# A linear-attention and gated feed-forward kernel: gate differences moved into the output product, two weight sums moved into slab 1, and batch 1's steps reordered

## The chip, the cores and the metric

The kernel runs on one core of a Trainium2 chip. The metric is the device time of one execution in microseconds (us). One profiled execution of each kernel gives a trace; the span in a trace is about 1.8 us shorter than the device time of the same run. The granted clock is the TensorE clock as the trace gives it: 1.00 is full speed, 0.50 half of it. The engines are TensorE (PE, with its weight loads PEld), VectorE (DVE), ScalarE (ACT), GpSimd (POOL) and the sync engine's DMA queue (SPq). "The Trainium skill" is the set of reference pages that is cited by page title below.

## The reference, cut to what matters

```python
# q, k, v: 8 batches x 8 heads x 576 x 64
q_s = softmax(q, over the 64 features)      # "norm": exp, sum, reciprocal, multiply
k_s = softmax(k, over the 576 positions)
kv  = einsum('bhsd,bhse->bhde', k_s, v)
x   = einsum('bhsd,bhde->bhse', q_s, kv)    # as 4608 tokens x 512
h   = x @ w_in                              # 512 -> 2048
g   = h / (1 + exp(-beta * h))
out = g @ w_out                             # 2048 -> 512
```

## The kernel before

The 4608 tokens are cut into 9 slabs of 512. In each slab, **pass 1** computes 16 gate tiles GT (TensorE: 4 matmuls each; ACT: the activation; DVE: a scale by 1/beta). The **output product** then multiplies GT with WOUT. From slab 1 on it does so with seven block products in place of eight (a Strassen-like scheme of 256-wide blocks): it needs sums (GS1, GS2) and differences of gate blocks, and sums and differences of weight blocks. Slab 0 uses the plain product, since the weights are only arriving. The attention of a later batch is woven between these matmuls ("ticks" count them). Names that come back in the profiles: EQ is exp(q), normalised in place; QT is EQ transposed; EQR and QTR are the same for the last 64 positions of each batch; KVD is the normalised kv product; XT is x, the operand of pass 1; TS holds the running sum of the first products; "PS" are PSUM banks, of which z5 and z2 are two.

The gate sums, all on DVE; `jobs` are GS1, GS2, and two differences written over GT:

```python
def g_sums(i0, n):                      # n pairs of tiles (i, i + 8)
    ...
    jobs = (
        (GS1[:, i0:i0 + n, :], g(i0, 0), g(i1, 1), ALU.add, ...),
        (GS2[:, i0:i0 + n, :], GT[:, i0:i0 + n, :], GT[:, i1:i1 + n, :], ALU.add, ...),
        (g(i0, 1), g(i0, 1), g(i0, 0), ALU.subtract, ...),
        (g(i1, 0), g(i1, 0), g(i1, 1), ALU.subtract, ...),
    )
    for o, a, b_, op, r, w in jobs:
        add(DVE, lambda e, ...: e.tensor_tensor(o, a, b_, op), r=r, w=w, war=True)
# in pass 1 of slabs 1 to 8, after tile n has been scaled:
if t and n in (8, 14, 16):
    g_sums(*{8: (0, 4), 14: (4, 3), 16: (7, 1)}[n])
```

The output product. `prod` is 16 matmuls of 256 columns, two for each gate pair, and `at(n)` runs hooks: loads, exponentials and norms of later batches. DVE's order is the order of this code.

```python
at(0)
prod(s, GS1, wsum(0)); prod(z5, gs2(0), wo(1, 1))
TS = PS[s]                                   # DVE
at(1)
TS -= PS[z5]                                 # DVE; frees bank z5 for the fourth product
at(2)
prod(z2, gs2(1), wo(0, 0))
TS -= PS[z2]                                 # DVE; frees bank z2 for the fifth
at(3)
prod(z5, gt(0, 0), wo(0, 1)); copy(z5, 0, 1, ACTE)
at(4)
prod(z2, gt(NG, 1), wo(1, 0)); copy(z2, 1, 0, ACTE)
at(5)
prod(z5, gt(0, 1), wsum(1)); last(z5, 1, 1)  # gt(0, 1) holds a difference
at(6)
prod(z2, gt(NG, 0), wsum(2)); last(z2, 0, 0) # gt(NG, 0) holds a difference
at(7)
```

(condensed; the bodies are cut.) `norm_turn` is a reduction and reciprocal on DVE, a multiply on GpSimd, then a DMA transpose QT<-EQ in the sync queue:

```python
if t == 1:
    on(0, w_diff, 0); on(0, exps, 2); on(0, load, 4); on(1, w_diff, 1)
    on(2, norm_main, 2, 0, 2, POOL)
    on(3, norm_main, 2, 2, 2, POOL)
elif t == 2:
    on(0, exps, 3); on(0, exp_qr)
    on(0, norm_turn, 3, 0); on(2, norm_turn, 3, 2)
    on(3, load, 5); on(3, load_rem, "qrf", qt_h, QRF, 4)
    on(4, exp_q, 4); on(4, casts, 4); on(5, exp_k, 4); on(5, exp_kr, 4)
    on(5, load, 6)
    on(6, norm_turn, 4, 0); on(7, norm_turn, 4, 2)
elif t + 2 < B:                              # slabs 3 to 5
    b = t + 2
    on(0, exps, b); on(0, casts, b)
    if b + 2 < B: on(0, load, b + 2)
    on(3, norm_turn, b, 0); on(4, norm_turn, b, 2)
```

The softmax here doesn't subtract the row's maximum and nothing guards it: scores larger than these inputs give would overflow.

## Time and profile before

| | before |
|---|---|
| device time, median of 3 runs (a fourth came with the result) | 298.32 us (297.19 to 298.73) |
| span of the trace | 296.9 us |
| TensorE busy | 271.1 us, 91% |
| DVE busy | 195.6 us, 66% |

TensorE is the engine that is nearly always busy, so what matters is what it waits for. The view of waits, engine PE, kernel before: who waited, on whose result, the total, how often, and the longest, in us.

```profile
PE PS L695 <- DVE GS L666: 12.4, 9, 2.0
PE PS L373 <- DVE EQ L333: 2.3, 2, 2.1
...
PE PS L695 <- DVE TS L749: 0.4, 1, 0.4
PE PS L373 <- POOL EQ L333: 0.4, 1, 0.4
PE PS L375 <- DMA QT<-EQ: 0.4, 1, 0.4
```

Most of what it waits is one thing: DVE's gate sums, 12.4 us in 9 waits, one in each slab from 1 to 8 (two in slab 3). The timeline of slab 5 shows how. Columns: start, busy time, engine, line, operation, output<-input, number of instructions; in brackets the idle time before and what ended it. TensorE, then DVE:

```profile
192.22 1.69 PE L695 MATMUL PS<-WSUM,GS 128*128 128x256 bf16 x14
195.81 0.39 PE L695 MATMUL PS<-WSUM,GS 128*128 128x256 bf16 x2 [1.90 <-DVE GS L666]
```

```profile
187.04 1.83 DVE L666 TENSOR_TENSOR GS<-GT 128x1024 bf16<-128x1024 bf16 x2
188.90 1.29 DVE L666 TENSOR_TENSOR GT<-GT 128x1024 bf16<-128x1024 bf16 x2
...
192.41 1.43 DVE L666 TENSOR_TENSOR GS<-GT 128x768 bf16<-128x768 bf16 x2
193.87 1.03 DVE L666 TENSOR_TENSOR GT<-GT 128x768 bf16<-128x768 bf16 x2
194.81 0.61 DVE L628 TENSOR_SCALAR GT<-GT,RB 128x512 bf16<-128x512 bf16 x2
195.46 0.63 DVE L666 TENSOR_TENSOR GS<-GT 128x256 bf16<-128x256 bf16 x2
```

The first product needs the GS1 of all eight pairs. TensorE does 14 of its 16 matmuls and stands still for 1.90 us before the last pair. The last activation of the slab ends at 193.11 us, but DVE is then in the burst for pairs 4 to 6. The differences of that burst (193.87, 1.03 us) stand in front of the last two scales and the last GS1, though nothing wants a difference before the sixth product.

The second loss is at the end of slab 0. The same views, kernel before, TensorE and DVE:

```profile
41.03 0.40 PE L373 MATMUL PS<-IDB,EQ 128*128 128x128 bf16 x4 [2.10 <-DVE EQ L333]
```

```profile
37.05 2.36 DVE L677 TENSOR_TENSOR WSUM<-WOUT 128x2048 bf16<-128x2048 bf16 x2 [4.93 <-DMA WOUT<-in_moe_w_out_dram]
39.33 0.68 DVE L331 TENSOR_REDUCE QS<-EQ 128x8 f32<-128x512 bf16 x1
```

Two w sums (2.36 us) wait for the last weights and stand ahead of batch 1's first reduction, and TensorE waits 2.10 us for the normalised EQ. The table by stretches gives the granted clock after that wait. Columns: stretch, its length, PE busy and its matmuls, granted clock (PEclk), DMA share, GB/s:

```profile
41.00:42.00 1.00, 0.96 (x8) 0.96 1.10 346
42.00:43.00 1.00, 0.96 (x3) 0.50 1.10 349
...
44.00:45.00 1.00, 1.00 (x4) 0.50 1.11 351
```

The clock is at 0.50 for about 3 us after TensorE has started again. This trace has a second such stretch, in slab 3, where TensorE had waited 1.96 us for gate sums until 133.14 us; it matters below, when slab 3 is compared:

```profile
134.00:135.00 1.00, 1.00 (x7) 0.54 0.61 141
135.00:136.00 1.00, 1.00 (x7) 0.50 1.09 151
```

### The profile page before, as it was taken

To read this page: it belongs to the slowest core of one execution; us is meant where nothing else is said; L and a number is where in the kernel's file an instruction comes from. 1 tells how busy PE (TensorE), PEld (TensorE's weight loads), DVE (VectorE), ACT (ScalarE), POOL (GpSimd) and SP (SyncE) were. 2 spreads that over 40 slices of the span, in tenths; PEclk is the share of its full clock that TensorE was granted. 3 is DMA by queue.
4 is the path that set the end of the run, shared out by engine and by line. 5 is a ranking of instruction groups with operands and counts; after the bars stand their busy time and mean duration, and the time that the engine had idled before them with its cause. 6 is when DMAs were issued, how large, how long until landed. Compare 5 with 4: busy or idle time off the path is not lost.

```text
span 296.9 us, 4679 instructions
## 1 busy us (share of the span) xinstructions
PE 271.1 (91%) x1820; PEld 169.4 (57%) x1845; DVE 195.6 (66%) x426; ACT 183.8 (62%) x282; POOL 62.9 (21%) x84
## 2 busy tenths in 40 slices
PE   8899979997999899979999799979998999899894
PEld 2444424446854685536755685568546845774483
DVE  5944295399757959795659774977488349625931
ACT  5787356998177978793467847784673477037510
POOL 2870013310800086300830072006000100000000
PEclk9999989999999999997999999999999999999999
DMA  7999999995970059999991044003500030002005
GB/s 227 302 206 194 258 354 348 239 369 189 338 204 0 0 94 334 296 281 228 337 269 61 2 98 171 0 1 81 186 2 0 20 141 0 2 35 106 2 2 140
DMA packets 57174, 45.40 MB, mean 153 GB/s; under 512 B 26416, under 2 KB 56128, under 8 KB 56128
## 3 DMA queue, kind: packets, MB, share of 16 engines
q1 hardware_dynamic: 52320, 40.38, 47.3%
q0 software_dynamic: 4224, 4.19, 8.5%
q10 hardware_dynamic: 608, 0.53, 0.5%
q8 instruction: 14, 0.23, 0.3%
q14 instruction: 8, 0.07, 0.1%
HBM read 36.71 MB, written 9.44 MB: 155 GB/s over the span
## 4 chain that ended last, share of the span: by engine, by line
PE 59%; DVE 23%; DMA 8%; POOL 3%; ACT 2%; SPq 2%; issue 2%; POOLq 0%; DVEq 0%
PE PS L375 32%; PE PS L695 27%; DMA WOUT<-in_moe_w_out_dram 7%; DVE GS L666 7%; DVE GT L628 4%; DVE GT L666 4%; DVE QS L331 2%; SPq L275 2%; ACT GT L622 2%; POOL EQ L333 1%; DMA QT<-EQ 1%; POOL WIN L543 1%; DVE WSUM L677 1%; DVE EQ L333 1%; DVE KVD L417 1%
## 5 line engine op out<-in xcount | busy, mean ns | idle before, releaser
L375 PE MATMUL PS<-XT,WIN 128*128 128x512 bf16 x560 | 129.5, 379 | 2.1 <-DVE XT L455 1.2
L622 ACT ACTIVATE GT<-PS,BETA 128x512 bf16<-128x512 f32 x144 | 98.7, 687 | 41.1 <-PE PS L375 40.9
L375 PEld LDWEIGHTS PS<-XT,WIN 128*128 128x128 bf16 x576 | 52.9, 98 | 60.9 <-DVE XT L455 2.6
L628 DVE TENSOR_SCALAR GT<-GT,RB 128x512 bf16<-128x512 bf16 x144 | 50.1, 374 | 38.1 <-ACT GT L622 37.9
L333 POOL TENSOR_TENSOR EQ<-EQ,QI 128x1024 bf16<-128x1024 bf16 (+1 forms) x16 | 27.0, 1690 | 127.3 <-DVE QI L332 126.9
L695 PE MATMUL PS<-WOUT,GT 128*128 128x256 bf16 x256 | 32.6, 273 | 0.4 <-DVE TS L749 0.4
L666 DVE TENSOR_TENSOR GS<-GT 128x1024 bf16<-128x1024 bf16 (+5 forms) x48 | 31.8, 704 | 0.8
L695 PE MATMUL PS<-WOUT,GS 128*128 128x256 bf16 x256 | 32.0, 280 | 0.2
L695 PE MATMUL PS<-WSUM,GT 128*128 128x256 bf16 x256 | 31.6, 273 | 0.1
L725 ACT COPY O2S<-PS 128x512 f32<-128x512 f32 x16 | 9.4, 584 | 35.2 <-PE PS L695 33.0
L695 PE MATMUL PS<-WSUM,GS 128*128 128x256 bf16 x128 | 17.0, 273 | 12.4 <-DVE GS L666 12.4
L695 PEld LDWEIGHTS PS<-WOUT,GS 128*128 128x128 bf16 x256 | 25.6, 100 | 4.3
L695 PEld LDWEIGHTS PS<-WOUT,GT 128*128 128x128 bf16 x256 | 24.9, 98 | 4.3 <-DVE TS L749 0.7
L695 PEld LDWEIGHTS PS<-WSUM,GT 128*128 128x128 bf16 x256 | 24.9, 98 | 3.7
L733 DVE TENSOR_TENSOR O2S<-TS,PS 128x512 f32<-128x512 f32 x16 | 11.0, 685 | 21.3 <-PE PS L695 21.3
L666 DVE TENSOR_TENSOR GT<-GT 128x1024 bf16<-128x1024 bf16 (+2 forms) x48 | 22.5, 510 | 0.8
L300 ACT ACTIVATE EQ<-QF 128x512 bf16<-128x512 f32 x32 | 17.7, 619 | 8.1 <-DMA QF<-in_q_dram 8.1
L375 PE MATMUL PS<-VB,EK 128*128 128x129 bf16 x128 | 22.1, 220 | 0.5 <-DVE VB L348 0.5
L695 PEld LDWEIGHTS PS<-WSUM,GS 128*128 128x128 bf16 x128 | 11.6, 98 | 17.8 <-DVE GS L666 14.9
L331 DVE TENSOR_REDUCE QS<-EQ 128x16 f32<-128x1024 bf16 (+1 forms) x20 | 19.8, 989 | 0.0
L455 ACT CAST XT<-PS 128x512 bf16<-128x512 f32 x18 | 10.3, 584 | 14.9 <-PE PS L375 11.1
L300 ACT ACTIVATE EK<-KF 128x512 bf16<-128x512 f32 x32 | 18.0, 620 | 0.0
(77 smaller groups left out, 227.8 us busy)
## 6 DMA issues: line engine op xcount, KB each, us to landing
out_dram<-O2S SPq DMA_DIRECT2D x8, 1024.0 KB, 4.3
QF<-in_q_dram SPq DMA_DIRECT2D x6, 1024.0 KB, 7.3
KF<-in_k_dram SPq DMA_DIRECT2D x6, 1024.0 KB, 10.2
VF<-in_v_dram SPq DMA_DIRECT2D x6, 1024.0 KB, 12.2
QF<-in_q_dram SPq DMA_DIRECT2D x4, 512.0 KB, 6.2
KF<-in_k_dram SPq DMA_DIRECT2D x8, 256.0 KB, 6.4
VF<-in_v_dram SPq DMA_DIRECT2D x8, 256.0 KB, 6.5
WIN<-in_moe_w_in_dram POOLq DMA_DIRECT2D x4, 512.0 KB, 7.2
```

Of the source, the lines that this page charges most:

```text
L275: add(SP, lambda e, h=h, a=a: e.dma_start(buf[64 * h:64 * h + 64, :, :], a), w=[(name, h)], slot=f"{name}{h}")
L300: add(ACTE, lambda e, o=o, a=a: e.activation(o, a, ACT.Exp), r=[(name + "f", i, hp)], w=[("e" + name, i, hp)])
L331: add(DVE, lambda e: e.tensor_reduce(s_, a, AX.X, ALU.add), r=ks, w=[("qs", i, hp0)])
L333: add(eng, lambda e: e.tensor_tensor(a, a, vb, ALU.mult), r=ks + [("qi", i, hp0)], w=ks)
L375: add(PE, lambda e: e.matmul(o, l, r_, start=start, stop=stop), r=r, w=w, bank=[bk])
L455: add(eng, lambda e: (e.copy if eng == ACTE else e.tensor_copy)(XT[i][:, hp, :], PS[bk][:, :]), r=[("ps", bk)], w=[("xt", i, hp)], bank=[bk])
L622: add(ACTE, lambda e: e.activation(GT[:, f, :], PS[bk][:, :], ACT.Silu, scale=BETA[:, f:f + 1]), r=[("ps", bk), "beta"], w=[("gt", f, 0), ...
L628: add(DVE, lambda e: e.tensor_scalar(GT[:, f, :], GT[:, f, :], RB[:, f:f + 1], None, ALU.mult), r=k + ["rb"], w=k)
L666: add(DVE, lambda e, o=o, a=a, b_=b_, op=op: e.tensor_tensor(o, a, b_, op), r=r, w=w, war=True)
L695: add(PE, lambda e, l=l, r_=r_, st=st, u=u, i=i: e.matmul(PS[bk][:, 256 * u:256 * u + 256], l, r_, start=st, stop=end and i == NG - 1, ski ...
L725: add(eng, lambda e: (e.copy if eng == ACTE else e.tensor_copy)(o, bank3(bk)), r=[("ps", bk)], w=w, bank=[bk])
L733: add(DVE, lambda e: e.tensor_tensor(o, ts, bank3(bk), ALU.add), r=["ts", ("ps", bk)], w=w, bank=[bk])
```

## The change

The intent: sums only in pass 1, in smaller bursts that end earlier (4, 2, 1 and 1 pairs); the differences as two operations of 128x2048 inside the output product, where DVE has gaps; the two w sums out of the way of batch 1's norms and into slab 1's pass 1; three of batch 1's four normalising multiplies on GpSimd; batch 1's steps at the ticks where their operands arrive; and batch 1's QF in quarters, started after the third WOUT chunk. The diff, cut to its core:

```diff
-        def g_sums(i0, n):          # GS1, GS2 and both differences, n pairs
+        def g_sum1(i, n): ...       # GS1 of n pairs
+        def g_sum2(i, n): ...       # GS2 of n pairs
+        def g_diff(fh):             # one difference, all 8 pairs: 128x2048
+            f, th = NG * fh, 1 - fh
+            add(DVE, lambda e: e.tensor_tensor(gv(f, th, NG), gv(f, th, NG), gv(f, 1 - th, NG),
+                                               ALU.subtract), ...)
@@ pass2_fast
             TS -= PS[z5]
+            g_diff(0)
             at(2)
             prod(z2, *gs2(1), *wo(0, 0), True)
             TS -= PS[z2]
+            g_diff(1)
             at(3)
@@ pass 1
-                    if t and n in (8, 14, 16):
-                        g_sums(*{8: (0, 4), 14: (4, 3), 16: (7, 1)}[n])
+                    for i_, w_ in {8: ((0, 4),), 12: ((4, 2),), 14: ((6, 1),), 16: ((7, 1),)}.get(
+                            n if t else 0, ()):
+                        g_sum1(i_, w_)
+                        g_sum2(i_, w_)
+                    if t == 1 and n in (4, 9):
+                        w_sum(2 * (n == 4))
@@ slab 0
-                todo = [(104 + 5 * hp, steps(t_steps, 1, (hp,), NOW, ACTE)) for hp in range(NHP)]
+                todo = [(x, steps(t_steps, 1, (hp,), NOW, ACTE))
+                        for hp, x in enumerate((98, 104, 109, 114))]
   ... (the ticks of exp_k, cast_v and kv_steps likewise; one kv step from the tail into the product)
-                load_main("qf", qt_h, QF, 1, split=2, after=P.writer[("wout", 7, 0)])
+                load_main("qf", qt_h, QF, 1, split=4, after=P.writer[("wout", 11, 0)])
-                w_sum(0)
-                w_sum(2)
-                    norm_main(1, hp, 1, POOL if hp % 2 else DVE)
+                    norm_main(1, hp, 1, POOL if hp else DVE)
```

More of the change, by code (lines that the diff above doesn't have):

```diff
@@ L647, in store8, with gv, gk, g_sum1 @@
                     r=[("o2", 0, 2 * th + u, dh) for u in range(2)], slot=f"outr{th}{dh}{h}")
-        def g_sums(i0, n):
-            def g(f, th):
-                return GT[:, f:f + n, 256 * th:256 * th + 256]
-            def gk(f, th):
-                return [("gt", f + x, th) for x in range(n)]
-            i1 = i0 + NG
-            jobs = (
-                (GS1[:, i0:i0 + n, :], g(i0, 0), g(i1, 1), ALU.add, gk(i0, 0) + gk(i1, 1),
-                 [("gs1", i0 + x) for x in range(n)]),
-                (GS2[:, i0:i0 + n, :], GT[:, i0:i0 + n, :], GT[:, i1:i1 + n, :], ALU.add,
-                 gk(i0, 0) + gk(i0, 1) + gk(i1, 0) + gk(i1, 1),
-                 [("gs2", i0 + x) for x in range(n)]),
-                (g(i0, 1), g(i0, 1), g(i0, 0), ALU.subtract, gk(i0, 0) + gk(i0, 1), gk(i0, 1)),
-                (g(i1, 0), g(i1, 0), g(i1, 1), ALU.subtract, gk(i1, 0) + gk(i1, 1), gk(i1, 0)),
-            )
-            for o, a, b_, op, r, w in jobs:
-                add(DVE, lambda e, o=o, a=a, b_=b_, op=op: e.tensor_tensor(o, a, b_, op),
-                    r=r, w=w, war=True)
+        def gv(f, th, n):
+            return GT[:, f:f + n, 256 * th:256 * th + 256]
+        def gk(f, th, n):
+            return [("gt", f + x, th) for x in range(n)]
+        def g_sum1(i, n):
+            add(DVE, lambda e: e.tensor_tensor(GS1[:, i:i + n, :], gv(i, 0, n), gv(i + NG, 1, n),
+                                               ALU.add),
+                r=gk(i, 0, n) + gk(i + NG, 1, n), w=[("gs1", i + x) for x in range(n)], war=True)
+        def g_sum2(i, n):
+            add(DVE, lambda e: e.tensor_tensor(GS2[:, i:i + n, :], GT[:, i:i + n, :],
+                                               GT[:, i + NG:i + NG + n, :], ALU.add),
+                r=[k_ for f in (i, i + NG) for th in range(2) for k_ in gk(f, th, n)],
+                w=[("gs2", i + x) for x in range(n)], war=True)
+        def g_diff(fh):
+            f, th = NG * fh, 1 - fh
+            add(DVE, lambda e: e.tensor_tensor(gv(f, th, NG), gv(f, th, NG), gv(f, 1 - th, NG),
+                                               ALU.subtract),
+                r=gk(f, 0, NG) + gk(f, 1, NG), w=gk(f, th, NG), war=True)
         def quarter(fh, dh):
@@ L784, in steps @@
                     return lambda: go(fn(*a))
-                todo = [(104 + 5 * hp, steps(t_steps, 1, (hp,), NOW, ACTE)) for hp in range(NHP)]
-                todo += [(106, one(exp_kr_s, 1))]
-                todo += [(110 + 5 * hp, one(exp_k, 1, hp, 1)) for hp in range(3)]
-                todo += [(122, steps(kv_steps, 1, (0,), NOW)), (126, steps(kv_steps, 1, (1,), NOW))]
-                todo += [(114, one(cast_v, 1, 0, DVE)), (115, one(cast_v, 1, 1, DVE)),
-                         (123, one(cast_v, 1, 2, DVE))]
+                todo = [(x, steps(t_steps, 1, (hp,), NOW, ACTE))
+                        for hp, x in enumerate((98, 104, 109, 114))]
+                todo += [(105, one(exp_kr_s, 1))]
+                todo += [(x, one(exp_k, 1, hp, 1)) for hp, x in enumerate((106, 110, 115))]
+                todo += [(x, one(cast_v, 1, hp, DVE)) for hp, x in enumerate((110, 114, 122))]
+                todo += [(x, steps(kv_steps, 1, (hp,), NOW))
+                         for hp, x in enumerate((116, 121, 126))]
             elif t < 3:
@@ L845, in bass_efficient_attn_shen__then__act_swish_beta_kernel @@
                 go(out_step(1, 0, NOW, ACTE))
-                go(kv_steps(1, (2,), NOW))
                 go(out_step(1, 1, NOW, ACTE))
```

## The prediction

> **What bounds it now.** TensorE is busy 91% of the 296.9 us span (page, busy shares), at a granted clock of 0.99. In every slab from 1 to 8 it stalls once before the last GS1 pair: the group "WSUM,GS" shows 12.4 us idle, all released by the DVE `GS` sums. By slab (TensorE waits per stretch): 1.3, 1.3, 2.1, 1.9, 1.9, 1.4, 1.3, 1.3. The timeline shows why: DVE does four-operation bursts (3.1 us for four pairs, 2.5 us for three), is behind when the last activation lands, and the last GS1 queues behind the 1.03 us of differences. The second loss is slab 0's output product: TensorE waits 2.1 us for batch 1's first normalised EQ, because two w sums (2.36 us) sit before its reduction, then runs at half clock for about 3.4 us (windows: 0.5 from 42 to 45 us).
>
> **Steady slabs (4 to 8).** Two 128x2048 differences should cost 1.22 us each, as the w sums do in the trace (the Trainium skill, "VectorE: DVE Perf Modes", side-by-side section, gives 1224 ns for this size at two elements a cycle; the trace agrees). That is 2.44 instead of 2.8 us, and it leaves the path: in the output product DVE has idle pieces of about 0.8, 0.8, 0.8 and 1.1 us, and the differences are first needed four products later. Replaying DVE's queue with trace durations, it has caught up at the last activation, and GS1 of the last pair comes about when TensorE arrives. Gain 1.75+1.75+1.3+1.25+1.25 = 7.3 us.
>
> **Slab 0.** No w sums before the norms; but batch 1's QF now waits for a later WOUT chunk (lands near 33.4 instead of 30.3 us). DMA is saturated either way, so the last QF lands near 39 us as before, its first quarter near 37. First transpose near 39.1 instead of 41.0, shorter stall, less half clock. Gain 2.3 us.
>
> **Slabs 1 to 3 give back.** Here DVE is full in the product: w differences (slab 1), norm reductions early (1.21 us each). Adding 2.44 us delays both TS subtractions, which release the banks of the 4th and 5th products, and the norms. Also the Trainium skill, "SBUF — State Buffer", section "SBUF: two separate sides", says a GpSimd operation and a two-input DVE operation exclude each other; the trace agrees (a 0.69 us multiply took 0.91 beside GpSimd's), so g_diff waits behind the 1.9 us GpSimd norm. Slab 1: about +2.5 against -0.8 gained. Slab 2: +2.3 against -1.3. Slab 3's first output matmul waits for QT<-EQ by DMA, queued behind about 24 us of saturated loads that start only after slab 2's second norm; that norm comes about 1.4 us later, so TensorE idles several us there, whatever slab 3's sums gain, and restarts at half clock, +1.5. Slabs 1 to 3 together: about +4.5.
>
> **Sum.** -7.3 -2.3 +4.5 = -5: 293.0 us, range 289.5 to 296.0. Chances: faster 0.38, same 0.60, slower 0.02.
>
> **What would show it.** Right: "WSUM,GS" idle falls from 12.4 to below 2.5 us; L666-type differences gone, two 1.2 us ones in each product; slabs 4 to 8 each 1.2 to 1.8 us shorter; slab 0 ends 2 to 3 us earlier. Wrong or right for the give-back: TensorE waits on DVE TS and on POOL EQ in slabs 1 and 2 of 2 us or more each, and a DMA QT<-EQ wait of 3 us or more in slab 3 with clock 0.5 after it.
>
> **What would make it wrong.** If the slab 1 to 3 waits overlap with slack that I count twice, the time goes to 289. If slab 0's later QF misses its transposes, or POOL's three serial multiplies (1.04 us each) pace TensorE, slab 0 gains nothing: 295.

## The result, and the profile after

| | before | changed |
|---|---|---|
| device time, median of 4 runs | 297.97 us (297.19 to 298.73) | 294.40 us (293.82 to 294.99) |
| ratio | | 0.9881, 95% interval 0.9845 to 0.9916 |
| span of the trace | 296.9 us | 292.3 us |
| TensorE busy | 91% | 93% |

A ratio is the mean time of one kernel's fast runs over that of the other's of the same rounds, so it is not quite the ratio of the two medians. The time fell by 3.6 us, 1.2%: inside the predicted range, and within 2%. The two traces differ by 4.6 us, 1 us more than the medians, since the traced run of the kernel before was a slow one of its kind (298.70 us); all differences by slab below are those of the two traces.

The view of waits, engine PE, changed kernel, against the same one of before:

```profile
PE PS L375 <- DMA QT<-EQ: 3.4, 1, 3.4
PE PS L373 <- POOL EQ L333: 2.6, 3, 1.5
PE PS L698 <- DVE TS L757: 2.0, 2, 1.3
PE PS L698 <- DVE GS L656: 1.9, 3, 0.8
PE PS L373 <- DVE EQ L333: 1.4, 1, 1.4
...
PE PS L698 <- DVE TS L752: 0.7, 1, 0.7
```

The wait for gate sums fell from 12.4 to 1.9 us, and 1.6 of these are in slab 1. In their place stand three that were 0.4 us each: the DMA transpose of QT (3.4), the GpSimd norm (2.6) and DVE's TS subtractions (2.7 in both lines).

The same slab 5, changed kernel, TensorE and DVE:

```profile
193.83 2.05 PE L698 MATMUL PS<-WSUM,GS 128*128 128x256 bf16 x16
```

```profile
195.14 0.29 DVE L656 TENSOR_TENSOR GS<-GT 128x256 bf16<-128x256 bf16 x1
...
198.26 1.22 DVE L668 TENSOR_TENSOR GT<-GT 128x2048 bf16<-128x2048 bf16 x1
...
200.59 1.22 DVE L668 TENSOR_TENSOR GT<-GT 128x2048 bf16<-128x2048 bf16 x1
```

All 16 matmuls of the first product run through. The last GS1 (195.14) comes 1.3 us after the product has begun and just before its last pair needs it. The two wide differences take 1.22 us each and lie behind the first and the second TS subtraction, where they hold up nothing. The length of each slab, from the first matmul of its pass 1 to that of the next (start of the first "XT,WIN" group in each timeline):

| slab | before us | changed us | difference |
|---|---|---|---|
| 0 (from 16.01 / 16.21) | 36.48 | 34.69 | -1.8 |
| 1 | 31.62 | 34.41 | +2.8 |
| 2 | 29.50 | 30.58 | +1.1 |
| 3 | 33.31 | 34.56 | +1.3 |
| 4 | 30.34 | 28.41 | -1.9 |
| 5 | 30.34 | 28.41 | -1.9 |
| 6 | 29.79 | 28.29 | -1.5 |
| 7 | 27.74 | 26.42 | -1.3 |
| 8 to the end of the span | 31.77 | 30.32 | -1.5 |

Slabs 4 to 8 gained 8.1 us, slab 0 gained 1.6 (its end moved from 52.49 to 50.90 us), and slabs 1 to 3 gave back 5.1. Slab 2 shows how. DVE, TensorE and GpSimd in its output product, changed kernel:

```profile
104.66 0.69 DVE L752 TENSOR_TENSOR TS<-TS,PS 128x512 f32<-128x512 f32 x1
105.26 1.88 DVE L668 TENSOR_TENSOR GT<-GT 128x2048 bf16<-128x2048 bf16 x1
107.06 1.21 DVE L331 TENSOR_REDUCE QS<-EQ 128x16 f32<-128x1024 bf16 x1
...
108.47 0.63 DVE L757 TENSOR_TENSOR TS<-TS,PS 128x512 f32<-128x512 f32 x1
109.02 2.67 DVE L668 TENSOR_TENSOR GT<-GT 128x2048 bf16<-128x2048 bf16 x1
```

```profile
105.41 1.26 PE L698 MATMUL PS<-WOUT,GT 128*128 128x256 bf16 x10 [0.74 <-DVE TS L752]
...
109.16 0.28 PE L698 MATMUL PS<-WOUT,GT 128*128 128x256 bf16 x1 [1.32 <-DVE TS L757]
```

```profile
104.16 1.90 POOL L333 TENSOR_TENSOR EQ<-EQ,QI 128x1024 bf16<-128x1024 bf16 x1 [20.28 <-DVE QI L332]
108.70 1.90 POOL L333 TENSOR_TENSOR EQ<-EQ,QI 128x1024 bf16<-128x1024 bf16 x1 [2.64 <-DVE QI L332]
```

The second TS subtraction (108.47) stands behind a wide difference of 1.88 us and a reduction of 1.21 us, and TensorE waits 1.32 us for its bank. The wait of 0.74 us before it is not the work of the differences: the first TS subtraction (104.66) stands in front of both. DVE had begun this product with a reduction that waited 1.45 us for ACT's exponential (until 102.50 us), and the 0.74 us are the same in a2, b4 and c2, where the differences come later. Both differences take longer than 1.22 us while a GpSimd multiply runs: the first one starts at 105.26, the multiply ends at 106.06, and the difference ends 1.08 us after that. The second norm's multiply starts at 108.70 us; before the change it started at 106.03.

In slab 3, the first output matmul waits for the DMA transpose, and the granted clock then drops. The half clock is no difference between the two traces, since slab 3 of the kernel before had one too (0.54 and 0.50, shown above); what differs is the wait for QT, 0.39 us before and 3.43 now, and the wait for gate sums, 2.13 us before and 0.28 now:

```profile
139.40 0.39 PE L375 MATMUL PS<-QT,KVD 128*128 128x512 bf16 x1 [3.43 <-DMA QT<-EQ]
```

```profile
139.00:140.00 1.00, 0.60 (x5) 0.95 1.26 306
140.00:141.00 1.00, 1.00 (x7) 0.50 1.04 385
...
142.00:143.00 1.00, 1.00 (x6) 0.50 0.94 197
```

### The profile page after: what moved, and what is told of

The parts are those of the page before. It is cut to its first block, busy times and chain, and to the rows that moved or that the text cites. A ratio compares the mean times of both kernels' runs of the same rounds, so it can differ in the third digit from the quotient of the medians.

```text
span 292.3 us, 4671 instructions
## 1 busy us (share of the span) xinstructions
PE 270.7 (93%) x1820; PEld 169.0 (58%) x1845; DVE 197.8 (68%) x409; ACT 183.8 (63%) x282; POOL 67.2 (23%) x85
## 4 chain that ended last, share of the span: by engine, by line
PE 69%; DVE 12%; DMA 9%; POOL 3%; ACT 3%; SPq 2%; issue 2%; POOLq 0%; DVEq 0%
PE PS L375 41%; PE PS L698 28%; DMA WOUT<-in_moe_w_out_dram 6%; DVE QS L331 3%; DVE GT L668 2%; POOL EQ L333 2%; DMA QT<-EQ 2%; SPq L275 2%; DVE GT L628 1%; ACT GT L622 1%; DMA QF<-in_q_dram 1%; DVE GS L661 1%; POOL WIN L543 1%; DVE QI L332 1%; DVE GS L656 1%
## 5 line engine op out<-in xcount | busy, mean ns | idle before, releaser
L628 DVE TENSOR_SCALAR GT<-GT,RB 128x512 bf16<-128x512 bf16 x144 | 52.5, 382 | 39.6 <-ACT GT L622 39.0
L333 POOL TENSOR_TENSOR EQ<-EQ,QI 128x1024 bf16<-128x1024 bf16 (+1 forms) x17 | 28.2, 1656 | 120.2 <-DVE QI L332 117.0
L698 PE MATMUL PS<-WOUT,GT 128*128 128x256 bf16 x256 | 33.3, 275 | 2.7 <-DVE TS L757 2.0
L668 DVE TENSOR_TENSOR GT<-GT 128x2048 bf16<-128x2048 bf16 x16 | 23.1, 1441 | 0.0
L661 DVE TENSOR_TENSOR GS<-GT 128x512 bf16<-128x512 bf16 (+2 forms) x32 | 22.7, 710 | 0.0
L348 POOL CAST VB<-VF 128x512 bf16<-128x512 f32 x25 | 18.0, 719 | 7.9 <-DMA VF<-in_v_dram 6.1
```

The source lines that it names most:

```text
L333: add(eng, lambda e: e.tensor_tensor(a, a, vb, ALU.mult), r=ks + [("qi", i, hp0)], w=ks)
L348: add(eng, lambda e: (e.copy if eng == ACTE else e.tensor_copy)(o, a), r=[("vf", i, hp), ("vone", i)], w=[("vb", i, hp)])
L628: add(DVE, lambda e: e.tensor_scalar(GT[:, f, :], GT[:, f, :], RB[:, f:f + 1], None, ALU.mult), r=k + ["rb"], w=k)
L661: add(DVE, lambda e: e.tensor_tensor(GS2[:, i:i + n, :], GT[:, i:i + n, :], GT[:, i + NG:i + NG + n, :], ALU.add), r=[k_ for f in (i, i + ...
L668: add(DVE, lambda e: e.tensor_tensor(gv(f, th, NG), gv(f, th, NG), gv(f, 1 - th, NG), ALU.subtract), r=gk(f, 0, NG) + gk(f, 1, NG), w=gk(f ...
L698: add(PE, lambda e, l=l, r_=r_, st=st, u=u, i=i: e.matmul(PS[bk][:, 256 * u:256 * u + 256], l, r_, start=st, stop=end and i == NG - 1, ski ...
```

## The experiments

Twelve runs follow, of ten new kernels and of two once more, in three calls; each call is one chip, on which the kernel before ran too. Theory Q, mine: what slabs 1 to 3 lose is the place of the wide differences in DVE's queue in slabs 1 and 2; they hold up the bank releases and the norms, and slab 2's second norm holds up the loads that stand ahead of slab 3's transposes in the sync queue. Its rivals: the two w sums in slab 1 (W), or a DMA queue that is full whatever slab 2 does (D).

### a1_early2: slab 2's differences back in pass 1

```diff
+                        if t == 2:
+                            g_diff(0, i_, w_); g_diff(1, i_, w_)   # after g_sum2, of the burst's pairs
@@ pass2_fast
-            g_diff(0)   and   g_diff(1)
+            if not (t == 2): g_diff(0)   and likewise g_diff(1)
```

> The changed kernel, with slab 2's gate differences put back into pass 1 beside its sums (all other slabs as changed). Theory Q (DVE's queue in slab 2's product delays the bank releases and the second norm, and through the norm the loads and slab 3's transposes): slab 2's two TS waits (2.0 us) go, a GS wait of about 1.3 us comes back, the second GpSimd norm of slab 2 ends about 2 us earlier against the start of the slab, the QT landing in slab 3 comes as much earlier, its wait falls from 3.4 to about 2 us; time about 2.3 us less than the changed kernel's 294.4, so 292. Rival D (the DMA queue's loads end when they end, whatever slab 2 does): the QT landing does not move, what slab 2 gains is waited again in slab 3, time 294.

Measured: 291.54 us, ratio 0.9792 (0.9754 to 0.9830). Slab 2 is 29.61 us (changed: 30.58), slab 3 is 32.41 (34.56). Both of slab 2's TS waits are gone and a GS wait of 1.3 us is back. The wait for QT hardly fell, to 3.1 us, because TensorE also came earlier; I had expected about 2. But the landing moved, and that is the point on which Q and D differ (it is put side by side with a2 below). The time itself proves less than it seems: this trace has no half clock in slab 3, and the changed kernel without it takes 32.16 us there (e1, below), so slab 3's 2.15 us are not the edit's. Against e1's trace the span is 0.8 us shorter, about what slab 2 gained; that 292 us came out as forecast is in part luck.

### a2_late12: the differences of slabs 1 and 2 behind the norms

```diff
             TS -= PS[z5]
-            g_diff(0)
+            if not (t < 3): g_diff(0)
             ...
             copy(z5, 0, 1, ACTE)
+            if t < 3: g_diff(0)
             ...
             copy(z2, 1, 0, ACTE)
+            if t < 3: g_diff(1)
```

> The changed kernel, with the two wide differences of slabs 1 and 2 moved behind the fourth and fifth product, so behind the TS subtractions and the norm reductions. Theory Q: the TS and POOL EQ waits in slabs 1 and 2 fall from 4.9 us to under 2; slab 2's second norm ends 2 us earlier; the QT wait in slab 3 does not grow; time 291 (3 to 4 us less than 294.4). Rival W (the loss in slab 1 is the two w sums now in its pass 1, not the differences): slab 1 keeps its length of 34.4 us, the time stays within 1 us of 294.4.

Measured: 288.17 us, ratio 0.9668 (0.9632 to 0.9704). Nothing is removed here, four operations stand later in one queue, and the time falls by about 6 us against the 294.4 of the first measurement, or 4 against the 292.0 of the last one (e1). Slab 1 takes 31.33 us instead of 34.41, slab 2 takes 29.40 instead of 30.58, slab 3 takes 33.52 instead of 34.56, with a half clock (0.50 from 135 to 138 us) as in the changed kernel's first trace. The waits for TS and POOL EQ, 5.3 us in the changed kernel's trace, are 1.5 us (this one's trace, view of waits: 0.7 and 0.8; the 0.7 is slab 2's first TS wait, which stays). Rival W alone would have left slab 1 as it was; it does not hold as the main cause.

The norm and the landing, from the timelines of four traces (start of the second GpSimd multiply of slab 2 plus its 1.90 us; start of the first output matmul of slab 3, which in all four waits for QT):

| kernel | second norm ends | first QT matmul | between |
|---|---|---|---|
| before | 107.93 | 137.54 | 29.6 |
| changed | 110.60 | 139.40 | 28.8 |
| a1_early2 | 109.21 | 137.92 | 28.7 |
| a2_late12 | 105.82 | 134.18 | 28.4 |

The landing follows the norm over 4.8 us of shifts, to within 1.3 us. That is what theory Q says, and rival D (a landing that does not move with slab 2) falls.

### a3_turn_first: batch 6's loads behind batch 4's transposes

```diff
-                on(5, load, 6)
                 on(6, norm_turn, 4, 0)
                 on(7, norm_turn, 4, 2)
+                on(7, load, 6)
```

> The changed kernel, with batch 6's loads queued behind batch 4's transposes in slab 2 instead of in front of them. If slab 3's wait for QT is the place of the transposes in the queue: that wait (3.4 us) is gone, TensorE does not fall to half clock there, slab 3 takes about 5 us less, time 289.5; slab 4 keeps its 28.4 us, since batch 6 is needed only at its end. If instead the transposes wait for the norm itself or for the engine, the wait stays above 2 us and the time above 293.

Measured: 291.15 us, ratio 0.9769 (0.9723 to 0.9816), so less than expected. The wait for QT is gone and slab 3 takes 28.97 us, 5.6 less than in the first trace of the changed kernel and 3.2 less than in e1's, which had no half clock. But slab 4, which I had said would keep its 28.41, takes 32.97. The sync queue and TensorE, this kernel:

```profile
118.97 5.94 SPq L482 DMA_TRANSPOSE QT<-EQ  x2
...
154.04 1.27 SPq L489 DMA_TRANSPOSE QTR<-EQR  x1
```

```profile
156.96 0.20 PE L375 MATMUL PS<-QTR,KVD 128*128 128x64 bf16 x1 [2.71 <-DMA QTR<-EQR]
```

Batch 4's transposes are now issued at 118.97 us (134.55 in the changed kernel), but the loads they overtook push batch 7's loads and with them slab 3's own transposes, so that QTR is late in slab 4. The same kind of wait moved one slab on, here with a half clock behind it (0.50 from 158 to 160 us). The trace is of the slowest of the four runs (292.72 us, the others 289.77 to 291.28). The place in the queue was the cause in slab 3; cured in one place only, most of it is lost again in another.

### a4_wsum_home: the two w sums back in slab 0

```diff
-                    if t == 1 and n in (4, 9):
-                        w_sum(2 * (n == 4))
@@ slab 0
                 exp_q(1)
+                w_sum(0)
+                w_sum(2)
```

> The changed kernel, with the two w sums back in slab 0, before batch 1's norms. Theory Q: WOUT's last chunk landed at 36.1 us, so the sums end near 38.6, slab 0's first norm comes about 1 us later and slab 0 is 0.5 to 1.5 us longer; slab 1's GS waits fall from 1.6 to about 0.3 us; the two cancel, time 294 to 295. Rival W (w sums in slab 1 are what it lost): slab 1 falls by 2 us or more, time 293 or less.

Measured: 293.41 us, ratio 0.9843 (0.9806 to 0.9880). Slab 0 takes 35.59 us (+0.9), slab 1 takes 32.58 (-1.8): slab 1's wait for gate sums (1.6 us) is gone, its waits for the norm (2.2) and TS (0.7) are unchanged. So W holds for 1.8 us of slab 1, which slab 0 gives back by half; the time is not clear of the changed kernel's.

### b1_only_gates and b2_only_slab0: the two halves of the change

b1 is the kernel before with the new sums and the wide differences; b2 is the kernel before with everything else.

```diff
# b1, against the changed kernel: slab 0 as before
+ w_sum(0), w_sum(2) after exp_q(1);  - the w_sum calls in slab 1's pass 1
+ split=2, after wout 7;  POOL if hp % 2 else DVE;  the old ticks
# b2, against the changed kernel: gates as before
+ g_sums(...) at n in (8, 14, 16), with both differences;  - g_diff(0), g_diff(1)
```

> The kernel before, with the gate part of the change alone (new sums and the two wide differences; slab 0, its loads and its w sums as before). Theory Q: slab 0 keeps 36.5 us, slab 1 takes about 32.6 (GS wait near 0.2, but TS and POOL waits of 2.5 to 3 us), slabs 2 and 3 about 30.6 and 34.3, slabs 4 to 8 together about 8 us less; time 293 to 294, ratio 0.985: so the whole gain of the change is the gate part and the slab 0 part nets about nothing. Rival: the slab 0 part carries its own 1.6 us, then this run is at 296.

> The kernel before, with everything but the gate part of the change (w sums in slab 1's pass 1, batch 1's norms on GpSimd, its steps by arrival, QF after the third WOUT chunk; sums and differences in pass 1 as before). Theory Q: slab 0 about 1.7 us less, slab 1 longer, because its pass 1 now holds 2.4 us of w sums on top of the differences (GS wait 3 us or more instead of 1.3), the rest as before: time 297.5 to 300, within 2% of before. Rival: the slab 0 part is worth 1.6 us by itself: 296.5.

Measured: b1 291.74 us, ratio 0.9777 (0.9736 to 0.9817), better than I had expected (slab 1, 32.59 us, is as forecast; slab 0 took 35.29 us instead of 36.5, since no half clock followed its wait of 2.01 us); b2 299.23 us, ratio 1.0040 (1.0020 to 1.0061). In b2 slab 0 falls by 1.9 us against before (36.48 to 34.61), and slab 1 grows by 2.7 (31.62 to 34.35), with waits of 2.7 us for gate sums and 0.6 for a w sum, and a half clock (0.50 from 70 to 73 us) that slab 1 of the kernel before did not have. So the rival for b2, 1.6 us won by slab 0's part alone, falls: the w sums cost in slab 1 what their absence saves in slab 0. That b1 seems 2.7 us faster than the whole change, more than b2's 1.2 us can explain, called for a repeat beside it.

### e1_change_again and e2_only_gates_again: the whole change and the gate part in the same rounds

No edit: the changed kernel, and b1's.

> The changed kernel once more, on the same chip and in the same rounds as the gate part alone: 294 us, ratio 0.988 (with the half clock in slab 3 in most runs), or down to 292.7 in runs that escape it.

> The gate part alone again, beside the whole change. If the slab 0 part costs about 1.2 us, as its own run against the kernel before says (1.0040), this is 1 to 2 us faster than the whole change on this chip: ratio near 0.980. If the 2.7 us between the two in the earlier calls was chance of clock and chip, the two agree within 0.5 us.

Measured: 291.96 us, ratio 0.9817 (0.9791 to 0.9843), and 292.37 us, ratio 0.9818 (0.9797 to 0.9839). They agree. The 2.7 us was not the slab 0 part: all four runs of the first measurement had a granted clock of 0.986 or 0.994, and three of the five in this one had 1.000 (291.50 to 291.96 us; the two at 0.994 took 292.85 and 292.93). This trace of the changed kernel has the same wait for QT, 3.22 us, and no half clock after it. Kernel e1_change_again, table by stretches:

```profile
139.00:140.00 1.00, 1.00 (x12) 1.00 1.17 414
140.00:141.00 1.00, 1.00 (x11) 1.00 1.34 393
```

Slab 3 then takes 32.16 us instead of 34.56, with the QT wait 0.2 us shorter. So the ratio of the change was 0.988 and 0.982; whether slab 3's wait is followed by the half clock is a part of that difference, and chip may be another. At equal clock the gain is clearest: in runs at 1.000 the kernel before took 297.18 and 297.32 us and the changed one 291.50 to 291.96. Its slab 0 part adds nothing that these runs can tell.

### d1_no_pool_norm: no GpSimd multiply in slabs 1 and 2 (wrong result)

```diff
+            if b in (2, 3):
+                return
             add(eng, lambda e: e.tensor_tensor(a, a, vb, ALU.mult), ...)
```

> Wrong result on purpose: the changed kernel without GpSimd's normalising multiply for batches 2 and 3 (the reductions and reciprocals stay). If the GpSimd multiply is what stretches the wide differences, all four in slabs 1 and 2 take 1.22 us as in slabs 4 to 8, instead of 1.22, 2.67, 1.88 and 2.67, and TensorE's TS waits in slabs 1 and 2 fall from 2.7 us to about 2 (the wait for the queue itself stays: reduction and difference before the second subtraction). If the stretch has another source (the operands, the DMA), the durations stay above 1.8 us.

One run, for its trace; the result is wrong, as said, and its 285.18 us are no claim. The four wide differences of slabs 1 and 2 in the changed kernel and in this one, DVE timeline:

```profile
71.86 1.22 DVE L668 TENSOR_TENSOR GT<-GT 128x2048 bf16<-128x2048 bf16 x1
...
74.96 2.67 DVE L668 TENSOR_TENSOR GT<-GT 128x2048 bf16<-128x2048 bf16 x1
...
105.26 1.88 DVE L668 TENSOR_TENSOR GT<-GT 128x2048 bf16<-128x2048 bf16 x1
...
109.02 2.67 DVE L668 TENSOR_TENSOR GT<-GT 128x2048 bf16<-128x2048 bf16 x1
```

```profile
71.79 1.22 DVE L670 TENSOR_TENSOR GT<-GT 128x2048 bf16<-128x2048 bf16 x1
...
74.89 1.21 DVE L670 TENSOR_TENSOR GT<-GT 128x2048 bf16<-128x2048 bf16 x1
...
102.61 1.22 DVE L670 TENSOR_TENSOR GT<-GT 128x2048 bf16<-128x2048 bf16 x1
...
105.71 1.21 DVE L670 TENSOR_TENSOR GT<-GT 128x2048 bf16<-128x2048 bf16 x1
```

The stretch is the GpSimd multiply's doing. TensorE's TS waits fall only from 2.7 to 2.0 us, as expected: the blocking accounts for 0.7 us of them, the order in the queue for the rest (0.74 us of which is slab 2's first TS wait, behind the reduction).

This trace also extends the table of shifts. Without the multiply, batch 3's transposes have no norm to wait for: the loads behind them start at 102.60 us instead of 111.91, batch 4's transposes are issued at 126.11 instead of 134.55, no wait for QT is left, and slab 3 takes 28.76 us.

### b3_qf7: QF released by the second WOUT chunk again

```diff
-split=4, after=P.writer[("wout", 11, 0)]
+split=4, after=P.writer[("wout", 7, 0)]
```

> The changed kernel, with batch 1's QF quarters released by WOUT's second chunk, as the halves were before, instead of its third. In the changed kernel TensorE waits 1.4 us for the first normalised EQ and ACT waited until 36.9 us for the first QF quarter. If the later release is what holds the first norm: the quarter lands near 35 us, the wait goes, slab 0 is 1.0 to 1.5 us shorter, time 293. If the copies only share one saturated DMA, the first quarter gains under 1 us and WOUT's last chunk lands later, with no wait for it: time within 0.7 us of 294.4.

Measured: 293.31 us, ratio 0.9838 (0.9794 to 0.9881), not clear of the changed kernel's 0.9817 to 0.9881. The issue of QF moved from 33.59 to 30.20 us (chain of waits), and the first quarter's exponential only from 36.87 to 36.50. Sharing with WOUT ate the head start; slab 0 took 34.55 us against 34.69.

### b4_all and c2_arrival: what the experiments point to

```diff
# b4: a2's late differences, and
-                on(5, load, 6)
+                on(7, load, 6)                       # behind norm_turn(4, 2)
-                    on(0, load, b + 2)
+                    on(7 if t == 3 else 0, load, b + 2)
-                    if t == 1 and n in (4, 9): w_sum(2 * (n == 4))
+                todo += [(115.5, one(w_sum, 2))]     # slab 0
                 go(out_step(1, 3, NOW, DVE))
+                w_sum(0)                             # end of slab 0
# c2: b4, and
-                        for hp, x in enumerate((98, 104, 109, 114))]      # transposes
+                        for hp, x in enumerate((104, 113, 117, 121))]
-                         for hp, x in enumerate((116, 121, 126))]         # kv products
+                         for hp, x in enumerate((123, 125, 127))]
```

> The changed kernel with the differences of slabs 1 and 2 late (as a2), batch 6's loads behind batch 4's transposes and batch 7's loads behind slab 3's transposes (so that the wait which a3 moved to slab 4's QTR does not come back), and the two w sums in slab 0's tail, one after the second cast and one after the last XT cast, where DVE stood idle for 1.2 and 1.9 us. Expected against a2's 288.2: slab 3 33.5 to about 29 us, slab 4 stays at 28.4, slab 1's GS wait of 1.3 goes: time 282 to 283.5, ratio about 0.948. If the DMA is simply too full in slabs 2 to 4 whatever the order, a wait of 2 us or more stays in slab 3 or 4 and the time is above 285.

> b4_all with batch 1's steps in slab 0's output product moved to where their operands arrive in the traces: transposes at ticks 104, 113, 117, 121 instead of 98, 104, 109, 114, the kv products at 123, 125, 127 instead of 116, 121, 126. In b4_all TensorE waited 1.8 us for the first normalised EQ at tick 98. If the stall is only a matter of order, it falls below 0.5 us and the time by about 1.2 us, from 283.7 to 282.5. If the chain behind it (the kv reciprocals, KVD and the XT casts at the end of slab 0) is what ends the slab, slab 0 keeps its 35 us and the time stays within 0.5 us of 283.7.

Measured: b4 283.73 us, ratio 0.9519 (0.9499 to 0.9540); c2 282.49 us, ratio 0.9487 (0.9467 to 0.9507). Both beat both kernels; b4 is just above the 282 to 283.5 us expected. In b4 slab 3 takes 29.15 us and slab 4 stays at 28.41, so the queue was not too full, it was in the wrong order; no DMA wait is among TensorE's. In c2 slab 0 takes 33.34 us (b4: 35.14) and the 1.8 us wait for the first EQ is gone. TensorE's longest waits that are left in c2 are 1.6 us for DVE's XT casts (in two), 1.2 for the very first operand of the kernel and 1.2 for KVD (in three).

## Why the prediction was right, and where its terms were off

- **Slabs 4 to 8: predicted -7.3, measured -8.1 us.** Right in mechanism and nearly in size: the GS wait did not merely shrink, it is zero in these slabs, where I had left up to 0.15 us.
- **The cost of a wide difference: predicted 1.22, measured 1.22 us** in slabs 3 to 8, where no GpSimd multiply stands beside it. The Trainium skill's "VectorE: DVE Perf Modes" gives 1224 ns for this size in its side-by-side section; the trace agrees.
- **Slab 0: predicted -2.3, measured -1.6 us by its end, -1.8 by its length.** This term was mis-sized, and most of what it did measure is the clock. The times that the prediction gave came out: the first quarter of QF at 36.84 us ("near 37"), the first transpose at 39.23 ("near 39.1"), and the wait for the first EQ fell from 2.10 to 1.40 us. But two waits appeared that were not there before, 0.33 us for a norm on GpSimd and 0.52 for ACT's XT cast, so that slab 0's waits inside the product fell only from 2.34 to 2.25 us. The rest is the half clock that did not come: in b1 the old slab 0 without it takes 35.29 us (before 36.48, changed 34.69), so about 1.2 us of the slab's 1.8 is the clock and 0.6 the change itself. The half clock followed in two of the three traces with the old slab 0 (before and e2, not b1) and in none with the new one, even after a4's wait of 2.30 us; that the shorter stall is what avoids it is not shown. The moved rate also dipped, to 182 GB/s from 37 to 38 us (387 before); in b3 it did not (369), and slab 0 was no shorter for it (34.55 us), so the dip is not what is missing.
- **Slab 1: predicted about +1.7 (2.5 less 0.8), measured +2.8 us.** The 0.8 that was to be gained was not: the GS wait is 1.6 instead of 1.3 us, because the two w sums stand in the same pass 1 (a4 removes that wait by taking them out). The TS and norm waits that the prediction named are there, 2.9 us together, and a2 shows their cause.
- **Slab 2: predicted +1.0 (2.3 less 1.3), measured +1.1 us.** Right in size. Of the two TS waits the differences cause only the second, 1.32 us, which a1 and a2 take away. "Delays both TS subtractions" was wrong for the first: it stands in front of the differences, and its 0.74 us stay in a2.
- **Slab 3: predicted a QT wait of 3 us or more and a clock of 0.5 after it; measured 3.43 us and 0.50** in the first trace. Right, and the shift table of a1 and a2 shows that the landing hangs on slab 2's second norm, a3 and b4 that it does so through the order in the sync queue. The prediction took the half clock for certain and for new; e1 shows that it is not certain, and slab 3 of the kernel before had one too. The +1.3 us is the longer QT wait (+3.0) less the gate-sum wait that went (-1.9), so the number fits without the half clock. With or without it, slab 3 of the changed kernel takes 34.56 or 32.16 us; between e1's runs at 0.994 and 1.000 on one chip the time differs by about 1 us.
- **Sum: predicted 293.0; measured 294.4 at first, 292.0 later.** The chances, 0.60 for within 2%, fit: the first ratio is 0.9881, the later 0.9817 (0.9791 to 0.9843, so across the 2%). Some of it is luck: the terms missed by -0.8 (slabs 4 to 8), +0.7 (slab 0) and +0.6 (slabs 1 to 3), which partly cancel, and each trace happens to have its own half clocks, two before and one changed.

What the gain was lost to, then: the moved work was not off the critical path there. Work moved out of pass 1 became waits in the two slabs where norm reductions stand between the TS subtractions, and one of these waits was handed on through GpSimd and the DMA queue to a slab that does not use that DVE time at all. The same operations two products later (a2) keep the gain.

What stays open: how much of slab 1's +2.8 us is due to the w sums and how much to the differences can't be added up, since a4 takes away 1.8 and a2 3.1; they overlap. The two halves do bound it: with the differences alone slab 1 takes 32.59 and 32.58 us (b1, e2; before 31.62), with the w sums alone 34.35 (b2, its half clock included). It also stays open when a wait is followed by the half clock.

## What to carry to other kernels

Moving work into an engine's gaps is priced by where it stands in that engine's in-order queue, not by how much of the gap it fills: put it after the last operation that releases a bank or starts another engine, and look at every stage, since a prologue's stages can be full where the steady ones have gaps. A delayed operation that releases a DMA queue is paid for by whoever stands at the end of that queue, here a slab later; when you change an order there, look for the wait that moves on (a3), and reorder all that stand behind it. Before you believe a difference of 1%, run both kernels in the same rounds, and before you compare one stage of two traces, look whether both have the same granted clock there.

## What the Trainium skill lacked or had wrong

- "TensorE: Matmul & The Clock Gate" (section "What's actually happening") gives a clock that halves after at least one idle window of about 3.4 us, with a free-running window. Here it halved after waits of 1.96 us (slab 3, before), 2.10 us (slab 0, before) and 3.43 us (slab 3, changed), and did not after 2.30 us (slab 0, a4), 3.14 us (slab 3, a1) and 3.22 us (slab 3, e1). So no length of wait separates the two in these traces. A free-running window would allow that one kernel shows both; no run here tests it. In slab 0 of the kernel before the drop came about 1 us after TensorE had started again at 41.03 us (0.96 in the window from 41 us, 0.50 from 42).
- "SBUF — State Buffer" (section "SBUF: two separate sides") says that a DVE operation with two SBUF inputs and a GpSimd operation exclude each other for a whole instruction. The runs agree and give the size: 1.22 us became 1.88 and 2.67 beside a GpSimd multiply of 1.90 us, and 1.22 again without it (d1). The page doesn't say that the operation that waits is recorded as busy; in these traces DVE's busy time contains the wait.
- "DMA: Bandwidth & Descriptors" (section "Queues, rings and completion order") says that on each DMA engine descriptors are consumed in ring order. The runs show a step before that, the order of issue on one engine, and not the order in a ring: a transpose put ahead of a batch's loads was issued at 118.97 instead of 134.55 us (a3). The page doesn't say what a full queue costs a small transfer behind it: here the transposes' data came 28.4 to 29.6 us after the event that let the loads in front of them start.
